# The kernels' transform of an attention + S4D program: its last stage on sixteen 32x32 tiles

## The chip, the cores and the metric

The program runs on one core of a Trainium2 chip. A core has five engines that run in parallel and each take their instructions in order: TensorE (PE in the profile, its weight loads PEld), VectorE (DVE), ScalarE (ACT), GpSimd (POOL) and SyncE (SP, which here only issues transfers). TensorE writes its results to PSUM, 128 partitions with eight banks of 512 float32 values each; DVE and ACT empty the banks. The metric is the device time of one execution in microseconds (us), lower is better.

## What is computed

The reference applies two kinds of layer in turn, each on a layer norm of x (2048 rows, 640 columns) and added to x: attention with 32 heads, and an S4D convolution; then both again with the same weights.

```python
A = -exp(log_A_real) + 1j * A_imag;  C = (C_real + 1j * C_imag) * dt[:, None]
P = exp((A * dt[:, None])[:, :, None] * pos)          # 640 channels, 128 states, 2048 positions
K = 2.0 * einsum("dn,dnl->dl", C, P).real             # one kernel of 2048 taps for each channel
y = irfft(rfft(u, 2L) * rfft(K, 2L))[:L] + u * D_skip # causal convolution, channel by channel
x = x + attn(norm(x)); x = x + s4d(norm(x)); x = x + attn(norm(x)); x = x + s4d(norm(x))
```

The convolution is done as a transform of u, a product with the transform of K, and a transform back. K does not depend on x, so its transform is made once and serves both S4D layers.

## The kernel before, in words

**The stages.** In order of time: the first attention (queries and keys are projected while the softmax runs; VectorE and TensorE build the taps K beside it, `kgen`, and store them in DRAM as `kd`); the output projection of the first attention (`out_proj`), with the transform of K (`ktransform`) in the same stretch; the first convolution (`ssm`); the second attention; the second convolution.

**What sets the order.** Inside the attention the order on every engine is written out by hand: a planner (`Plan`, `fill`, `slot`, `weave`) keeps a clock for TensorE, ScalarE and VectorE and ties each instruction to the one before it. `weave` takes steps of `kgen` (a step ends at each `yield`) while the planned VectorE is not ahead of the planned TensorE by 0.2. Some small steps wait in a list `slow`; each has a number k and is taken at the latest when `expand(k)` begins. Outside the attention, so in `out_proj`, `ktransform` and `ssm`, no such ties are made: a list scheduler orders the instructions when the program is built, those written earlier first where several are ready, and each engine then runs its list in order. `ktransform` is written between the two halves of row 2 of `out_proj` (the call `weave(1000)`), so its instructions come ahead of those of the rows behind.

**`out_proj`.** Sixteen rows s of 128 positions. A row is loaded (`otl`), split in two parts (`oh` by ScalarE, `ol` by VectorE), multiplied by the two parts of the weights in 30 matmuls of 320 columns (tile `po`, two banks `M`), added to x, normed, and cut into `uh` and `ul`, which the convolution reads.

**`ktransform`.** Five blocks b of 128 channels, one after the other:

1. The taps of the block, `kl` (128 x 2048), come from `kd` in one transfer of 1 MB, a block ahead, into one of two buffers. The skip weight is added to tap 0. Sixteen transposes (tile `pkt`, two banks `T`) turn it; ScalarE writes the high part `ktrh` (scaled by `ksc`), VectorE the low part `ktrl`.
2. Eight groups of twelve matmuls with the constants `e1` (tile `pkx`, two banks `X`), each copied into `kx1` (`x1` in the code; ScalarE six, VectorE two). The copies lay four channels side by side.
3. The last stage, in eight steps q: four transposes of `kx1` (`pkt`), ScalarE writes `kxt` with the scale, one 128x128 matmul of 512 columns with the constant `f2` (tile `pkf`, two banks `F`), and VectorE takes its result apart with two `stream_shuffle`s: the first sixteen rows of each 32 twice into `kn0`, the second sixteen twice into `kn1`; ScalarE then gives half of `kn1` the other sign (`sgn`). After every second step two transfers of 512 KB store `kn0` in `kha` and `kn1` in `khb` (DRAM).

So `kha` and `khb` hold each half of the result doubled: the convolution multiplies its own transform by the one, and its transform with rows exchanged (`SWAP`) by the other.

**`ssm`.** For each block of channels eight steps q; in `stage2b` a step loads `ka` and `kb` (256 KB each, from `kha` and `khb`, one piece of 2 KB for each partition; three buffers) and VectorE and GpSimd multiply by them.

**Bound.** The scale `ksc` is made once from the largest absolute values of C and the skip weights: three `reduce_max` on VectorE into `kbig` (written in one step of `kgen`, with the end of the first `expand`), one `partition_all_reduce` on GpSimd, and seven small VectorE instructions (`bound`).

Of the kernel before, what the change touches and what calls it, by code (L numbers as in the profile page):

```python
# [21 lines left out]
P = 128  # L22
L = 2048
# [64 lines left out]
def mha_s4d_kernel(ctx, tc, x_in, wqkv, wo, lar, aim, cr, ci, ldt, dsk,  # L88
                   c_e1, c_eb, c_f2, c_fa, c_sel, c_lv, c_id, c_sg, c_e16, c_f16, c_id16, c_dn, out, parts="asas", general=None):
# [22 lines left out]
    def pst(pool, *a, **k):  # L112
        return ps_[pool].tile(*a, **k)
# [4 lines left out]
    kha = dram.tile([P, D // 4, P], F32, name="kha")  # L118
    khb = dram.tile([P, D // 4, P], F32, name="khb")
# [72 lines left out]
    def kgen():  # L192
# [166 lines left out]
        for n, t in enumerate((ld["cr"], ld["ci"], skip)):  # L359
            ve.reduce_max(big[:, n:n + 1], t, axis=AX.X, apply_absolute_value=True)  # L360
# [12 lines left out]
        slow.append((1, bound))  # L373
        load_powers(2)
        yield
# [815 lines left out]
    ups = []  # L1191
# [17 lines left out]
    DUP0 = list(range(16)) * 2  # L1209
    DUP1 = list(range(16, 32)) * 2  # L1210

# [3 lines left out]
    def ktransform(e1):  # L1215
# [4 lines left out]
        f2 = c1.tile([P, P], F32, name="f2")  # L1220
        sy.dma_start(f2, c_f2)
        sgn = c1.tile([P, 1], F32, name="sgn")
        sy.dma_start(sgn, c_sg)

        skip = c1.tile([P, NCT], F32, name="skip")
        sy.dma_start(skip, dsk)

        def load(b):
            kl = c2.tile([P, L], F32, name="kl")
            sy.dma_start(kl, kd[b * P:b * P + P, :])  # L1230
            return kl
        kls = [load(0)]

        def unit_load(b):
            kl = kls.pop()
            if b + 1 < NCT:
                kls.append(load(b + 1))
# [3 lines left out]
            for i4 in range(4):  # L1241
                pt = pst("T", [P, 4, P], F32, tag="T", name="pkt")
# [6 lines left out]
            x1 = c1.tile([P, 32, NI // 2, 16], F32, name="kx1")  # L1249
            for i2 in range(NI // 2):  # L1250
# [6 lines left out]
                (ve.tensor_copy if i2 % 4 == 1 else se.copy)(by_channel(x1, i2), ps.rearrange("p r i (g c) -> p (r i) g c", c=4))  # L1257
                yield
            prev = None
            for q in range(9):  # L1260
                if q < 8:
                    pt = pst("T", [P, 4, P], F32, tag="T", name="pkt")
                    for g in range(4):
                        te.transpose(pt[:, g, :], x1[:, 4 * q + g].rearrange("p i s -> p (i s)"), ident)
                    xt = c2.tile([P, 512], F32, name="kxt")
                    se.activation(xt, pt.rearrange("p g k -> p (g k)"), AF.Copy, scale=ksc[:, 1:2])
                if prev is not None:
                    g0 = b * 32 + 4 * (q - 1)
                    if q % 2:
                        kn = [c2.tile([P, 2, 512], F32, name=f"kn{s}") for s in range(2)]  # L1270
                    px = pst("F", [P, 512], F32, tag="F", name="pkf")
                    te.matmul(px, f2, prev, start=True, stop=True)  # L1272
# [3 lines left out]
                    if q % 2 == 0:  # L1276
                        for s, dst in enumerate((kha, khb)):
                            sy.dma_start(dst[:, g0 - 4:g0 + 4, :].rearrange("p g k -> p (g k)"),
                                         kn[s].rearrange("p q k -> p (q k)"))
                prev = xt  # L1280
                yield
        for b in range(NCT):
            yield from unit_load(b)
# [65 lines left out]
    def ssm(x, uh, ul, consts, last):  # L1349
# [19 lines left out]
        with ExitStack() as c:  # L1369
# [29 lines left out]
            def stage2b(b, q, xt):  # L1399
# [3 lines left out]
                sy.dma_start(ka, kha[:, g0:g0 + 4, :].rearrange("p g k -> p (g k)"))  # L1403
                sy.dma_start(kb, khb[:, g0:g0 + 4, :].rearrange("p g k -> p (g k)"))
# [227 lines left out]
def _constants():  # L1632
# [13 lines left out]
    for s, o, m in ((0, 0, C), (1, 0, S), (0, 1, -S), (1, 1, C)):  # L1646
        fa[:, s, :, :, o] = np.einsum("hli,cd->hlcid", m.reshape(4, 4, 16), e4)
    f2 = f2.reshape(2, NI // 2, 2, 4, P).transpose(1, 0, 2, 3, 4)
    sg = np.zeros((4, 2, 16, 1))
    sg[:, 0], sg[:, 1] = -1.0, 1.0  # L1650
# [5 lines left out]
    cs = dict(c_e1=e1.reshape(P, -1), c_eb=eb.reshape(P, -1), c_f2=f2.reshape(P, P), c_sg=sg.reshape(P, 1),  # L1656
              c_fa=fa.reshape(P, -1), c_sel=sel.reshape(P, -1), c_lv=lv, c_id=np.eye(P))
    cs = {n: np.ascontiguousarray(a.astype(np.float32)) for n, a in cs.items()}
    for n, a in (("c_e16", e1), ("c_f16", f2)):
# [11 lines left out]
          "c_e1", "c_eb", "c_f2", "c_fa", "c_sel", "c_lv", "c_id", "c_sg",  # L1671
# [31 lines left out]
```

## Time and profile before

| | |
|---|---|
| time, median of 3 runs (lowest to highest) | 2678.65 us (2678.31 to 2682.86) |
| the profiled execution: its time, its span | 2680.85 us, 2679.1 us |
| busy in the span: PE, ACT, DVE, POOL | 94%, 88%, 57%, 31% |
| first attention ends, `out_proj` begins | about 1103 us into the span |
| first to last transpose of `kl`; last shuffle of `pkf` | 1133.4 to 1229.7 us; 1249.5 us |
| first matmul of the first convolution | 1273.6 us |
| last load of `ka` in the second convolution | 2653.9 us |

Times in the answers of the trace are microseconds from the start of the span, and mean times of one instruction are in nanoseconds (ns). In a row of a group stand line, engine, operation, what is written and what is read, shapes and count, then busy time and the mean of one, then the idle time of the engine just before them. Line 78 is the wrapper through which the ScalarE, VectorE, GpSimd and SyncE calls go, so such rows are told apart by their tiles. In a timeline, "x16" means sixteen instructions of one kind in a row, with the start of the first and the time to the end of the last. A float32 matmul appears as two instructions, one for each pass. The ends of matmuls are modelled, so it is the distance from start to start that tells what one costs.

### The profile page before, as it was taken

The numbers are of one execution on the slowest core, as the hardware profiler recorded it, in microseconds if no ns is written. First come the engines' busy times: TensorE is split into PE (matmuls) and PEld (weight loads), VectorE is DVE, ScalarE is ACT, GpSimd is POOL, SyncE is SP. The second block draws the span as 40 slices with busy tenths as digits, with TensorE's granted clock in tenths as the row PEclk, the third lists the DMA queues.
The fourth block names the chain that finished last, engine by engine and source line by source line (L and its number), as shares of the span: only waits on it lengthen the run. The fifth ranks groups of instructions, "written<-read, shape, count | busy, mean of one in ns | idle before, by whom it ended". The sixth has DMA issues, their size and how long they took to land.

```text
span 2679.1 us, 116332 instructions
## 1 busy us (share of the span) xinstructions
PE 2530.0 (94%) x51106; PEld 1425.0 (53%) x51106; DVE 1516.0 (57%) x3451; ACT 2368.7 (88%) x2793; POOL 827.7 (31%) x1256
## 2 busy tenths in 40 slices
PE   7899999999999998899998999999999998999898
PEld 3445444444444443678896444454444443444788
DVE  8687777886855994477776333232233221154865
ACT  7889999999999999676655799999999999999564
POOL 1123323333323334301672122222222222222376
PEclk9999999999999999999999999999999999999999
DMA  6513222322221224364542121121121113222465
GB/s 210 181 49 86 67 76 55 87 55 76 52 61 49 54 68 155 110 233 162 189 151 69 40 59 50 50 58 47 45 65 38 54 30 93 69 67 60 145 190 162
DMA packets 186580, 242.18 MB, mean 90 GB/s; under 512 B 43376, under 2 KB 128976, under 8 KB 184400
## 3 DMA queue, kind: packets, MB, share of 16 engines
q1 hardware_dynamic: 150048, 188.35, 21.8%
q0 software_dynamic: 36016, 46.30, 7.0%
q8 instruction: 403, 6.60, 1.0%
q14 instruction: 113, 0.93, 0.1%
HBM read 158.50 MB, written 76.01 MB: 88 GB/s over the span
## 4 chain that ended last, share of the span: by engine, by line
ACT 52%; PE 25%; issue 10%; DVE 6%; DMA 3%; POOL 1%; SPq 0%; ACTq 0%; DVEq 0%; POOLq 0%
ACT pt L78 50%; PE pa L892 4%; PE psv L1419 3%; PE psy L1429 3%; PE S L858 3%; PE psx L1407 2%; PE m L611 1%; PE psx L1384 1%; PE po L1312 1%; DMA kop<-ks 1%; PE pst L1394 1%; PE pkf L1272 1%; DVE ktab L78 1%; PE po L1307 1%; PE pq L764 1%
## 5 line engine op out<-in xcount | busy, mean ns | idle before, releaser
L78 ACT ACTIVATE pt<-S 128x1024 f32<-128x1024 f32 x2048 | 1928.6, 1032 | 41.4 <-PE S L858 29.2
L892 PE MATMUL pa<-pt,V 64*32 64x512 f32 x16384 | 1100.9, 590 | 1.4 <-DVE oc L78 1.2
L858 PE MATMUL S<-qop,kop 61*32 61x512 f16 x16384 | 882.9, 381 | 85.2 <-ACT pt L78 68.4
L858 PEld LDWEIGHTS <-kop 61*32 61x32 f16 x16384 | 366.7, 89 | 741.1 <-issue 622.4
L892 PEld LDWEIGHTS pa<-pt,V 64*32 64x32 f32 x16384 | 315.1, 106 | 74.6 <-issue 9.7
L78 POOL DMA_DIRECT2D dn<-oc x252 | 124.5, 501 | 670.6 <-DVE oc L78 643.8
L78 DVE TENSOR_SCALAR qc<-m 128x512 f32<-128x512 f32 (+1 forms) x68 | 46.8, 689 | 303.6 <-PE m L611 303.6
L78 POOL DMA_DIRECT2D db<-dn x252 | 128.0, 514 | 135.1 <-DMA dn<-dr 132.1
L78 DVE COPY oc<-pa 128x512 f32<-128x512 f32 x64 | 44.1, 690 | 199.6 <-PE pa L892 191.9
L611 PE MATMUL m<-xh,wh 64*32 64x512 f16 x2560 | 147.9, 379 | 5.5 <-DVE qc L78 5.5
L78 POOL DMA_DIRECT2D ot<-oc x256 | 130.4, 516 | 71.6 <-DVE oc L78 42.8
L611 PE MATMUL m<-xh,wl 64*32 64x512 f16 x2560 | 148.1, 377 | 0.0
L611 PE MATMUL m<-xl,wh 64*32 64x512 f16 x2560 | 146.7, 376 | 0.0
L611 PEld LDWEIGHTS <-wh 64*32 64x32 f16 x5120 | 92.9, 93 | 78.4 <-issue 36.4
L78 ACT COPY xt<-pst 128x1024 f16<-128x1024 f16 x80 | 81.6, 1022 | 47.2 <-PE pst L1394 47.0
L1412 POOL TENSOR_TENSOR t<-t,kb 128x512 f32<-128x512 f32 x80 | 102.0, 1276 | 67.6 <-DVE t L78 66.7
L78 POOL DMA_DIRECT2D dn<-dr x63 | 35.3, 560 | 248.8 <-DVE dr L78 236.4
L78 DVE TENSOR_SCALAR V<-m 128x160 f32<-128x160 f32 x64 | 20.7, 324 | 158.5 <-PE m L577 158.5
L78 DVE TENSOR_TENSOR kb<-ktab 128x512 f32<-128x512 f32 x160 | 107.7, 692 | 0.0
L577 PEld LDWEIGHTS <-xh 128*128 128x128 f16 x960 | 79.7, 98 | 47.0 <-issue 31.6
L1413 POOL TENSOR_TENSOR t<-t,t 128x512 f32<-128x512 f32 x78 | 99.3, 1273 | 8.5 <-DVE t L78 2.6
L329 PEld LDWEIGHTS m<-kb,ka 128*32 128x32 f32 x3840 | 61.0, 109 | 72.1 <-issue 55.3
(305 smaller groups left out, 4020.7 us busy)
## 6 DMA issues: line engine op xcount, KB each, us to landing
ka<-kha SPq DMA_DIRECT2D x80, 256.0 KB
kb<-khb SPq DMA_DIRECT2D x80, 256.0 KB
db<-dn POOLq DMA_DIRECT2D x252, 64.0 KB, 2.6
kop<-ks SPq DMA_DIRECT2D x176, 80.0 KB
kpw<-wd POOLq DMA_DIRECT2D x60, 192.0 KB, 4.7
qop<-qs SPq DMA_DIRECT2D x256, 40.0 KB
ot<-oc POOLq DMA_DIRECT2D x256, 40.0 KB, 3.0
kha<-kn SPq DMA_DIRECT2D x20, 512.0 KB
```

The source lines that it names most:

```text
L78: made = f(out, *a, **k)
L329: chain(te.matmul(ps[32 * j:32 * j + 32, c8, :], a[n][:, ch, :], b[n][:, dd, :], start=(n == 0), stop=(n == 2), tile_position=(0, 32 * j)))
L577: chain(te.matmul(ps[:, :n], a_[:, ct, sl], m[:, ct, :], start=(k == 0), stop=(k == 14)))
L611: chain(te.matmul(ps[r][32 * t:32 * t + 32, :], a_[rows, ct, 32 * u:32 * u + 32], m[rows, ct, 512 * v:512 * v + 512], start=(k == 0), stop ...
L764: te.matmul(pq, a_[:, ct, :], m[:, ct, sl], start=(n == 0), stop=(n == 14))
L858: chain(te.matmul(S[32 * t:32 * t + 32, 512 * r:512 * r + 512], kt_[rows, kc + 32 * t:kc + 32 * t + 32], qt[rows, :], start=True, stop=Tru ...
L892: chain(te.matmul(pa[r][32 * j:32 * j + 32, :], V[rows, kt, VP * h:VP * h + 32], pts[j // 2][rows, 512 * (j % 2):512 * (j % 2) + 512], sta ...
L1407: te.matmul(px, f2[:, f, :], xt[:, k, :], start=(n == 0), stop=(n == 2))
L1412: ge.tensor_mul(t2, t2, kb)
L1413: (ge if g0 else ve).tensor_add(t1, t1, t2)
L1419: te.matmul(pv[:, g].rearrange("p r i c -> p (r i c)"), t1[:, g * P:g * P + P], fa, start=True, stop=True)
L1429: te.matmul(py[:, i, :], eb[:, 4 * i4 + i, r, :], v[:, r, 4 * i4 + i].rearrange("p g c -> p (g c)"), start=(r == 0), stop=(r == 1))
```

## The change

- **Last stage of `ktransform`.** `kx1` is laid out so that the channels of one residue (channel modulo 4) have 32 partitions of the transposed tile to themselves. `f2` becomes two 32x32 matrices for each group of 32 rows: one gives the first half of the result already doubled, the other the second half doubled and with its signs. `turned(t)` makes the sixteen transposes of half a block (now in the banks `X`, shared with `pkx`; each reads with a step of 32 elements) and four ScalarE writes of `kxt`. `ends(t, xt, s, dst)` issues sixteen 32x32 matmuls of 512 columns, four row groups times four column groups, into four banks (`F0` to `F3`, one buffer each), two copies by VectorE and two by ScalarE into `kn`, and two transfers of 512 KB. It is called four times a block. The two shuffles, the ScalarE sign and the constant `sgn` with its load are gone; the banks `T` are gone in this stretch.
- **`kl`.** One buffer instead of two, allocated with the projection weights; the first block is loaded while the first attention still runs, each later one after the sixteen transposes of the block before, in four transfers of 32 channels each (256 KB), which put the channels in the new order. The skip weights are loaded in that order too.
- **`kha`, `khb`** change layout, so `ka` and `kb` are read in pieces of 512 bytes, four for each partition, instead of one of 2 KB.
- **Bound.** A `yield` before each of the three `reduce_max`; `bound` stands behind the loads of `load_powers(2)` in `slow`, with number 3 instead of 1.

```diff
         for n, t in enumerate((ld["cr"], ld["ci"], skip)):
+            yield
             ve.reduce_max(big[:, n:n + 1], t, axis=AX.X, apply_absolute_value=True)
...
-        slow.append((1, bound))
         load_powers(2)
+        slow.append((3, bound))
...
+            kl0[:] = [w1.tile([P, L], F32, name="kl")]
+            rest.append(lambda: load_kl(0))
...
+    def load_kl(b):
+        for ch in range(4):
+            sy.dma_start(kl0[0][32 * ch:32 * ch + 32, :],
+                         kd[b * P:b * P + P, :].rearrange("(g c) l -> c g l", c=4)[ch])
...
-                pt = pst("T", [P, 4, P], F32, tag="T", name="pkt")
+                pt = pst("X", [P, 4, P], F32, tag="X", name="pkt")
...
+            if b + 1 < NCT:
+                load_kl(b + 1)
-            x1 = c1.tile([P, 32, NI // 2, 16], F32, name="kx1")
+            x1 = c1.tile([P, 4, NI // 2, 4, 32], F32, name="kx1")
...
-                    te.matmul(px, f2, prev, start=True, stop=True)
-                    for s in range(2):
-                        ve.stream_shuffle(kn[s][:, (q - 1) % 2, :], px, [DUP0, DUP1][s])
-                    se.activation(kn[1][:, (q - 1) % 2, :], kn[1][:, (q - 1) % 2, :], AF.Copy, scale=sgn)
...
+            def turned(t):
+                xt = c2.tile([P, 4, 4, P], F32, name="kxt")
+                for q in range(4):
+                    pt = pst("X", [P, 4, P], F32, tag="X", name="pkt")
+                    for g in range(4):
+                        te.transpose(pt[:, g, :], x1[:, :, :, :, 16 * t + 4 * q + g].rearrange("p c i s -> p (c i s)"), ident)
+                    se.activation(xt[:, q], pt, AF.Copy, scale=ksc[:, 1:2])
+                return xt
+
+            def ends(t, xt, s, dst):
+                px = [pst("F", [P, 512], F32, tag=f"F{ch}", name=f"pkf{ch}") for ch in range(4)]
+                for ch in range(4):
+                    rows = slice(32 * ch, 32 * ch + 32)
+                    for g in range(4):
+                        te.matmul(px[ch][32 * g:32 * g + 32, :].rearrange("p (q k) -> p q k", k=P), f2[rows, s, :],
+                                  xt[rows, :, g, :], start=True, stop=True, tile_position=(32 * ch, 32 * g))
+                for h in range(2):
+                    kn = c2.tile([P, 2, 4, P], F32, name=f"kn{s}")
+                    for ch in range(2):
+                        (se.copy if ch else ve.tensor_copy)(kn[:, ch], px[2 * h + ch].rearrange("p (q k) -> p q k", k=P))
+                    sy.dma_start(dst[2 * b + t][:, 2 * h:2 * h + 2], kn)
+            xts = [turned(0)]
+            for t in range(2):
+                yield
+                ends(t, xts[t], 0, kha)
+                yield
+                if t == 0:
+                    xts.append(turned(1))
+                yield
+                ends(t, xts[t], 1, khb)
...
-                sy.dma_start(ka, kha[:, g0:g0 + 4, :].rearrange("p g k -> p (g k)"))
-                sy.dma_start(kb, khb[:, g0:g0 + 4, :].rearrange("p g k -> p (g k)"))
+                for t, src in ((ka, kha), (kb, khb)):
+                    sy.dma_start(t.rearrange("p (g k) -> p g k", k=P),
+                                 src[g0 // 16].rearrange("(g a) c q k -> (a c) g q k", g=4)[:, :, q % 4])
...
-                    psum(c3, M=2, T=2, F=2)
+                    psum(c3, M=2, F=1)
```

More of the change, by code (lines that the diff above doesn't have):

```diff
@@ L88, in mha_s4d_kernel @@
 def mha_s4d_kernel(ctx, tc, x_in, wqkv, wo, lar, aim, cr, ci, ldt, dsk,
-                   c_e1, c_eb, c_f2, c_fa, c_sel, c_lv, c_id, c_sg, c_e16, c_f16, c_id16, c_dn, out, parts="asas", general=None):
+                   c_e1, c_eb, c_f2, c_fa, c_sel, c_lv, c_id, c_e16, c_f16, c_id16, c_dn, out, parts="asas", general=None):
     nc = tc.nc
@@ L117, in mha_s4d_kernel @@
     wd = dram.tile([P, 3, len(LV), D], F32, name="wd")
-    kha = dram.tile([P, D // 4, P], F32, name="kha")
-    khb = dram.tile([P, D // 4, P], F32, name="khb")
+    kha = dram.tile([2 * NCT, P, 4, 4, P], F32, name="kha")
+    khb = dram.tile([2 * NCT, P, 4, 4, P], F32, name="khb")
     qs = dram.tile([2, D, L], F16, name="qs")
@@ L1219, in ktransform @@
         c2 = c.enter_context(tc.tile_pool(name="f2", bufs=2))
[L1220 to L1223, printed above, removed]
+        f2 = c1.tile([P, 2, 32], F32, name="f2")
+        sy.dma_start(f2, c_f2.rearrange("p (s m) -> p s m", s=2))
         skip = c1.tile([P, NCT], F32, name="skip")
[L1226 to L1232, printed above, removed]
+        sy.dma_start(skip, dsk.rearrange("(g c) n -> c g n", c=4))
+        kls = kl0
         def unit_load(b):
-            kl = kls.pop()
-            if b + 1 < NCT:
-                kls.append(load(b + 1))
+            kl = kls[0]
             ve.tensor_add(kl[:, 0:1], kl[:, 0:1], skip[:, b:b + 1])
@@ L1260, in unit_load @@
-            for q in range(9):
-                if q < 8:
-                    pt = pst("T", [P, 4, P], F32, tag="T", name="pkt")
+            def turned(t):
+                xt = c2.tile([P, 4, 4, P], F32, name="kxt")
+                for q in range(4):
+                    pt = pst("X", [P, 4, P], F32, tag="X", name="pkt")
                     for g in range(4):
[L1264 to L1272, printed above, removed]
-                    for s in range(2):
-                        ve.stream_shuffle(kn[s][:, (q - 1) % 2, :], px, [DUP0, DUP1][s])
-                    se.activation(kn[1][:, (q - 1) % 2, :], kn[1][:, (q - 1) % 2, :], AF.Copy, scale=sgn)
[L1276 to L1280, printed above, removed]
-                yield
```

18 lines of the change are left out of this document (9 added, 9 removed).

## The prediction

> **What bounds the kernel now.** First the page: its first line and its line of engines.
>
> ```profile
> span 2679.1 us, 116332 instructions
> PE 2530.0 (94%) x51106; PEld 1425.0 (53%) x51106; DVE 1516.0 (57%) x3451; ACT 2368.7 (88%) x2793; POOL 827.7 (31%) x1256
> ```
>
> Those are averages over unlike stages, so next the busy times by stretch around the change (columns: PE, PEld, DVE, ACT, POOL, granted clock, DMA share, GB/s): projection rows alone, rows with the kernels' transform, the rest of the rows, the first convolution.
>
> ```profile
> 1103.00:1133.00 30.00, 28.30 (x184) 26.92 (x184) 21.44 (x54) 11.78 (x17) 15.34 (x22) 1.00 0.49 154
> 1133.00:1248.00 115.00, 113.34 (x927) 86.86 (x927) 87.55 (x238) 89.10 (x145) 6.34 (x6) 1.00 0.56 212
> 1248.00:1289.00 41.00, 37.79 (x348) 35.30 (x347) 31.73 (x84) 23.70 (x40) 10.03 (x7) 1.00 0.41 141
> 1289.00:1416.00 127.00, 125.32 (x1312) 111.61 (x1311) 92.93 (x223) 77.65 (x144) 99.64 (x79) 1.00 0.50 158
> ```
>
> In the transform's 115 us PE is busy for 113, VectorE and ScalarE for three quarters. The chain that ended last says the same: the transform's matmuls, and then rows of the projection with nothing else between them.
>
> ```profile
> 1238.45 0.86 PE pkf L1272 x2
> ...
> 1248.20 2.92 PE po L1312 x20
> 1251.12 1.58 PE po L1307 x10
> ```
>
> So work taken from PE here should shorten the stage, as long as rows can be pulled into the time that comes free: the rows after 1248 were ready to run but stood behind the transform.
>
> **The last stage, what goes.** Two views: PE's timeline inside block 1's last stage, and the groups of the 115 us.
>
> ```profile
> 1170.00 1.02 PE L1272 MATMUL pkf<-kxt,f 128*128 128x512 f32 x2
> 1170.86 0.60 PE L1264 MATMUL pkt<-ident,kx 128*128 128x128 f32 x4
> 1171.30 1.08 PE L1272 MATMUL pkf<-kxt,f 128*128 128x512 f32 x2
> ```
>
> ```profile
> L1272 PE MATMUL pkf<-kxt,f 128*128 128x512 f32 x80 | 41.3, 608 | 0.0
> L78 ACT ACTIVATE kn<-kn,sgn 128x512 f32<-128x512 f32 x38 | 27.0, 721 | 1.5 <-DVE kn L78 0.9 <-DVE va L78 0.2
> L78 ACT ACTIVATE kxt<-pkt,ksc 128x512 f32<-128x512 f32 x40 | 26.6, 677 | 8.8 <-PE pkt L1264 8.8
> L78 ACT COPY kx<-pkx 128x512 f32<-128x512 f32 x30 | 17.4, 584 | 6.4 <-PE pkx L1256 6.3
> L78 DVE STREAM_SHUFFLE kn<-pkf 128x512 f32<-128x512 f32 x77 | 52.2, 737 | 0.0
> L78 DVE COPY kx<-pkx 128x512 f32<-128x512 f32 x10 | 6.9, 686 | 3.2 <-PE pkx L1256 3.2
> ```
>
> A step takes 1.30 us of PE: 0.86 for the two passes of the matmul (its start to the next transposes), 0.44 for four transposes (1170.86 to 1171.30). The matmuls that go are 5 blocks x 8 x 0.86 = 34.4 us. The 160 transposes stay; that they now read with a step I cost at nothing, and a tenth on each (0.011 us) would be 1.8 us.
>
> **What comes.** Twenty calls of `ends`, each sixteen float32 tiles of 512 columns. The trace has no such call; the nearest are the attention's matmuls on eight 64x32 tiles, and one sum over four 32x32 tiles.
>
> ```profile
> 791.56 1.04 PE L892 MATMUL pa<-pt,V 64*32 64x512 f32 x16
> 792.42 0.40 PE L858 MATMUL S<-qop,kop 61*32 61x512 f16 x8
> 792.76 0.24 PE L577 MATMUL m<-vh,xh 128*128 128x160 f16 x1
> ...
> 793.18 0.23 PE L577 MATMUL m<-vh,xh 128*128 128x160 f16 x1
> 793.25 0.23 PE L577 MATMUL m<-vl,xh 128*128 128x160 f16 x1
> 793.41 0.41 PE L858 MATMUL S<-qop,kop 61*32 61x512 f16 x8
> 793.64 1.04 PE L892 MATMUL pa<-pt,V 64*32 64x512 f32 x16
> ...
> 155.66 0.40 PE L539 MATMUL m<-sq,sel 32*32 32x512 bf16 x4
> 155.98 0.89 PE L858 MATMUL S<-qop,kop 61*32 61x512 f16 x16
> ```
>
> Eight float32 tiles (sixteen instructions, two passes each) take 0.86 us together, the time of one: tiles run side by side. Four 32x32 tiles in four row groups do too: 0.32 us to the next kind, about one pass of 0.23. And changing between tile shapes costs: from the scores to another tiled kind 0.23 us, to a 128x128 kind 0.34; from 128x128 back 0.16 instead of the 0.07 between two of its own. So about 0.1 us each way. An estimate for one `ends`: 0.86, some 0.1 for starting twice as many tiles, 0.2 for two changes of shape: 1.15 us, and 23.0 for twenty. **PE saves 34.4 - 23.0 = 11.4 us.** Bounds: 15 if calls stand together and change no shape; -4 if no more than eight tiles ever run side by side (20 x (1.72 + 0.2) = 38.4). I take the estimate, since rows and columns of tiles each show no loss.
>
> The Trainium skill (TensorEngine Tiling (Array Packing), Key Properties) says that a change of tiling mode drains TensorE, which speaks against small groups of tiles between 128x128 work. Taken at its word, each of forty changes would cost the tail of a matmul, 0.608 less the 0.43 between two passes, 0.18 us, and 7 us in all; the rows above show a change at half of that, 4 us, and the sum goes by them.
>
> **What empties the banks.** VectorE loses 80 shuffles of 0.737 (59 us) and gets 40 copies of 0.686 (27); ScalarE loses 40 signs of 0.721 (29) and gets 40 copies of 0.584 (23). Both were behind PE, so this is worth nothing by itself. But the banks are single now. After an `ends` two copies an engine must end, about 1.4 us, before the next `ends` may write. Of the three such waits in a block the first is covered by the sixteen transposes of `turned(1)` (1.8 us); two are bare: 2.8 us. And `ends` needs all four writes of `kxt`: 4 x 0.677 plus 0.6 for the first transposes, 3.3 us, of which the transposes fill 1.8: 1.5 bare. Together 4.3 us a block, **22 us in all, if nothing else is put there**. What can be put there is row matmuls (25 us of them stand after 1248: 2.92 + 1.58 for each row) and the next block's transposes. I take 3 us lost, with 0 and 22 as ends: rows were ready, and the scheduler did put them into the gaps of the present order.
>
> **Loads and stores.** `kl` in four transfers waits for the block's transposes and lands while 96 matmuls and the last stage run, some 20 us; price 0 (if that cover went, each block would wait for 1 MB). On SP it stands ahead of the stores of `kn` and the loads `otl`; four issues of 0.4 us delay them by 1.6 us, against two row buffers. The constant `sgn` leaves SP just ahead of `skip`, for which the first block waits:
>
> ```profile
> 1130.03 0.61 SPq L78 DMA_DIRECT2D sgn<-in_c_sg  x1
> ```
>
> **-0.6 us** (0 to -0.6). `ka` and `kb` in 512-byte pieces: the packets of a row load (all of 512 bytes, two microseconds from 1133) against those of `ka` and `kb` (20 us from 1360), and the lead of one load over its use.
>
> ```profile
> q1 hardware_dynamic: 656, 0.33, 54.7%
> ...
> q1 hardware_dynamic: 1612, 2.94, 46.1%
> ```
>
> ```profile
> 1334.45 0.32 SPq L78 DMA_DIRECT2D kb<-khb  x1
> 1334.87 0.38 SPq L78 DMA_DIRECT2D ka<-kha  x1
> ```
>
> ```profile
> 1342.57 0.67 DVE L78 TENSOR_TENSOR t<-psx,ka 128x512 f32<-128x512 f32 x1
> ```
>
> 0.547 x 2 us x 16 / 656 = 27 ns for 512 bytes; 0.461 x 20 x 16 / 1612 = 92 ns for, mostly, 2 KB. A pair of loads becomes 1024 x 27 ns / 16 = 1.7 us, against a lead of 7.7 us (the same number in both orders). Price 0; each 0.1 us that the 80 pairs came late would be 8 us.
>
> **The bound.** On the attention's start ScalarE, its bottleneck, waits for scores that wait for VectorE, and the three maxima lie on that chain.
>
> ```profile
> 133.58 1.52 DVE kbig L78 x3
> ```
>
> ```profile
> 138.03 1.02 ACT L78 ACTIVATE pt<-S 128x1024 f32<-128x1024 f32 x1 [4.78 <-PE S L858]
> ```
>
> With the `yield`s the planner can put the emptying of `m` first. Worth up to 1.5 us of ScalarE's 4.8; I take **1.0** (0 to 1.5), as the planner's clock does not know that VectorE was late.
>
> **The sum**: 11.4 - 3 + 0.6 + 1.0 = 10.0 us less. The profiled execution took 2680.85 (span 2679.1 and 1.75 around it), 2.2 above the median; against it the forecast is 2670.85, against the median of 2678.65 it is 2668.7.
>
> **The rivals.** What a measurement can tell from no change is 0.2%, 5.4 us: 2673.3 to 2684.0.
>
> 1. *The waits stay empty (slower).* The scheduler sets the order before the run. If it takes the sixteen tiles for sixteen matmuls in a row, PE looks full to it, it lines up the four `ends` of a block and puts no row between; on the chip PE then stands idle at `pkf`, and the rows come after as now. Price: all 22 us, so 2678.65 + 22 - 11.4 - 1.6 = 2687.7. It decides from 13 us of empty waits on. For it: the attention, full of such tiles, is ordered by hand with a clock of its own. Against: nothing in the present order shows a misjudged stretch, but nothing in it is tiled either.
> 2. *ScalarE takes over the last stage.* It has 8 x 0.677 + 8 x 0.584 = 10.1 us a block there, PE had 8 x 1.30 = 10.4. If that stage stays as long as ScalarE and nothing moves in, the gain is 5 x 0.3 = 1.5 us and 1.6: 2675.5. For it: the bare waits; against: ScalarE is busy for only 89 of 115 us. The Trainium skill (TensorEngine Tiling (Array Packing), PSUM Bottleneck) speaks for this one: tiling speeds up TensorE and leaves the emptying of PSUM as it was.
> 3. *Only eight tiles run side by side*: 2678.65 + 4 + 3 - 1.6 = 2684. Against it stand the rows above; sixteen float32 tiles are not among them.
> 4. *The short pieces come late*: slower by 8 us and more; the leads speak against it.
>
> **How the numbers follow.** Forecast 0.52, rival 1 0.26, rival 2 0.15, rival 3 0.04, rival 4 0.03. The time is the forecast's, 2668.7, with its own range of 2662 to 2674 (waits of 0 to 8 us, 15 us saved at most). The range of 8 in 10 reaches over rivals 2 and 3 to just beyond rival 1: 2660 to 2689. Faster: the forecast but for its edge, and a little of rival 2, 0.53; within: most of rival 2, half of rival 3 and the part of rival 1 near its turning point, 0.19; slower 0.28.
>
> **What would show it.** In the profile after: the sixteen-tile groups `pkf` start within 0.1 us and the next kind 1.1 to 1.2 us later (wrong, if 1.9 or more); the waits of PE for copies out of `pkf` add up to 3 us (rival 1: over 13); the rows left after the last `ends` take no longer than now; the first convolution starts 9 us earlier after the attention; no wait for `ka` or `kb`; ScalarE's gap near 135 us is 3.3 to 4.8 us. The prediction is wrong if the stage from the attention's end to the convolution does not shorten, or if the attention or the convolutions move by more than 2 us.

## The result, and the profile after

The kernel after takes 2701.09 us (median of 5 runs, 2695.70 to 2704.51), the kernel before, run beside it, 2679.00 us (2678.31 to 2682.86). The ratio is 1.0076, with a 95% interval of 1.0061 to 1.0091: slower by 0.8%. The forecast was 2668.7 us, and the range ended at 2689.

The first line of the page after and its line of engines:

```profile
span 2699.3 us, 117384 instructions
PE 2534.6 (94%) x51666; PEld 1422.0 (53%) x51666; DVE 1487.5 (55%) x3331; ACT 2365.6 (88%) x2793; POOL 824.5 (31%) x1256
```

VectorE and ScalarE have lost work as expected, PE has not. The busy times by stretch, cut at the same events as for before (rows alone, rows with the transform, the other rows, first convolution; columns as there, the granted clock after POOL):

```profile
1104.20:1134.20 30.00, 27.73 (x181) 26.38 (x180) 20.92 (x53) 11.75 (x17) 15.39 (x22) 1.00 0.50 153
1134.20:1269.40 135.20, 120.76 (x1516) 87.75 (x1516) 67.35 (x129) 88.64 (x149) 8.65 (x7) 0.97 0.56 187
1269.40:1306.70 37.30, 34.08 (x328) 31.43 (x321) 28.66 (x74) 21.05 (x36) 7.55 (x5) 1.00 0.48 159
1306.70:1433.70 127.00, 125.35 (x1312) 111.63 (x1311) 93.00 (x224) 77.65 (x144) 99.40 (x79) 1.00 0.54 159
```

The transform's stretch is 20 us longer, with PE idle for 14.4 us in it (1.7 before) and the granted clock below one. The first convolution is unchanged: 125.35 us of PE in 127, against 125.32. PE's timeline in block 0's last stage shows the new groups and where they stand:

```profile
1150.72 1.14 PE L1274 MATMUL pkf<-kxt,f 32*32 32x512 f32 x32
1151.80 1.16 PE L1265 MATMUL pkt<-ident,kx 128*128 128x128 f32 x8
1152.89 1.04 PE L1274 MATMUL pkf<-kxt,f 32*32 32x512 f32 x2
1153.86 0.71 PE L1265 MATMUL pkt<-ident,kx 128*128 128x128 f32 x4
1154.50 1.13 PE L1274 MATMUL pkf<-kxt,f 32*32 32x512 f32 x30
1156.45 1.60 PE L1274 MATMUL pkf<-kxt,f 32*32 32x512 f32 x32 [0.81 <-DVE kn L78]
1158.36 1.69 PE L1274 MATMUL pkf<-kxt,f 32*32 32x512 f32 x32 [0.32 <-DVE kn L78]
```

The first group runs as forecast: the next kind starts 1.08 us after it. The order puts the last four transposes behind the first tile of the second group; they wait for a bank that ScalarE empties into `kxt`, and the group's rest waits with them. The second, third and fourth then stand one behind the other with no row between; the third and the fourth wait for the copies out of the single banks, and even a group that has begun is stretched to 1.6 us, because its later tiles find their bank still full. The groups of the stretch say the same, with the idle time before each:

```profile
L1274 PE MATMUL pkf<-kxt,f 32*32 32x512 f32 x640 | 33.9, 614 | 5.7 <-DVE kn L78 4.1 <-ACT kn L78 1.6
L1265 PE MATMUL pkt<-ident,kx 128*128 128x128 f32 x160 | 24.7, 292 | 3.4 <-ACT kxt L78 3.4
L1241 PE MATMUL pkt<-ident,kl 128*128 128x128 f32 x80 | 13.5, 306 | 5.8 <-DVE ktrl L78 5.0 <-DVE kl L78 0.9
L78 DVE COPY kn<-pkf 128x512 f32<-128x512 f32 x39 | 25.6, 687 | 40.1 <-PE pkf L1274 30.6 <-DMA khb<-kn 5.9 <-issue 3.6
L78 ACT COPY kn<-pkf 128x512 f32<-128x512 f32 x39 | 21.7, 587 | 18.3 <-PE pkf L1274 7.7 <-DMA khb<-kn 6.1 <-ACT kn L78 4.5
```

Twenty groups are busy for 33.9 us where 20 x 1.14 = 22.8 would do: 11 us are waits inside them (0.9 of it is half clock in one group, see the last section). With the 14.4 - 1.7 = 12.7 us of idle time that is 24 us lost, against the 11.4 saved. Three causes in these rows were in no step of the prediction. VectorE and ScalarE wait 12 us for the stores of `kn` (two buffers for each). PE waits for `ktrl`, which stands behind those copies (ahead of the wait for it near 1164, VectorE stands 2.1 us for a store). And PE waits for `kxt`, which stands on ScalarE behind the `u` and `uh` of the rows and two copies of `kn`. The chain shows such a store on the path, and then the rows that stood behind the transform as before:

```profile
1212.67 5.36 DMA khb<-kn
...
1270.44 2.93 PE po L1321 x20
```

### The profile page after: what moved, and what is told of

Its sections match the earlier page's. It is cut to its first block, busy times and chain, and to the rows that moved or that the text cites. A ratio compares the mean times of both kernels' runs of the same rounds, so it can differ in the third digit from the quotient of the medians.

```text
span 2699.3 us, 117384 instructions
## 1 busy us (share of the span) xinstructions
PE 2534.6 (94%) x51666; PEld 1422.0 (53%) x51666; DVE 1487.5 (55%) x3331; ACT 2365.6 (88%) x2793; POOL 824.5 (31%) x1256
## 4 chain that ended last, share of the span: by engine, by line
ACT 51%; PE 26%; issue 10%; DVE 5%; DMA 4%; POOL 1%; SPq 0%; ACTq 0%; DVEq 0%; POOLq 0%
ACT pt L78 49%; PE pa L893 4%; PE S L859 3%; PE psv L1429 3%; PE psy L1439 2%; PE psx L1417 2%; PE m L612 2%; PE po L1321 2%; PE psx L1393 1%; PE pst L1403 1%; PE pkx L1255 1%; PE po L1316 1%; DMA kop<-ks 1%; PE pkt L1265 1%; PE pq L765 1%
```

## The experiments

The theories, by the numbers that the expectations use. **Theory 1**: the order puts the groups back to back on single banks and leaves the rows for later. A **rival**: the stores of `kn` hold up the copies. Another: the tiles or the changes of shape cost it themselves. **Theory 3** came with the first results: ScalarE does the rows' `u` and `uh` ahead of the copies. Ten of the kernels below are changes of the kernel after, two of the kernel before, and one is the kernel after once more. To compare them within one execution the table gives the **stage**: from the first row matmul of the first projection (`po`) to the last `psx` group of the first convolution. Its two ends are the first start in the row of the tile `po` and a row of PE's timeline; in the kernel after, 1104.0 and 1429.04. The ratio is to the kernel before, run beside each (medians 2679.0 to 2680.2 us). One profile was taken of each kernel, so a stage is one execution, and two of one program differ by 4.5 us (after and after again).

| kernel | time, us | ratio to before, 95% interval | stage, us |
|---|---|---|---|
| before (first runs) | 2678.65 | | 308.4 |
| after | 2701.09 | 1.0076 (1.0061 to 1.0091) | 325.0 |
| after, again | 2700.81 | 1.0082 (1.0068 to 1.0095) | 329.5 |
| after, edit of bound undone | 2696.56 | 1.0059 (1.0045 to 1.0074) | 326.6 |
| before, only the edit of bound | 2680.72 | 1.0001 (0.9992 to 1.0010) | 308.4 |
| after, half of the stores left out | 2698.37 | 1.0056 (1.0042 to 1.0070) | 324.1 |
| after, u on VectorE | 2693.83 | 1.0054 (1.0040 to 1.0067) | 323.6 |
| before, u on VectorE | 2682.39 | 1.0010 (1.0000 to 1.0020) | 310.8 |
| order by hand | 2710.59 | 1.0102 (1.0086 to 1.0118) | 335.8 |
| order by hand, u on VectorE | 2687.66 | 1.0029 (1.0019 to 1.0038) | 311.6 |
| the same, pieces of four | 2678.15 | 0.9994 (0.9985 to 1.0003) | 306.2 |
| the same, pieces of three | 2689.07 | 1.0035 (1.0023 to 1.0048) | 315.1 |
| pieces of four, pkx divided | 2681.06 | 0.9999 (0.9991 to 1.0008) | 307.5 |
| the same, edit of bound undone | 2679.31 | 0.9996 (0.9987 to 1.0006) | 307.2 |
| fewer, larger pieces, edit of bound undone | 2675.53 | 0.9982 (0.9973 to 0.9991) | 301.1 |

**The order by hand.** The transform gives way after each piece, the row matmuls from the seventh row on are tied into PE's order with it, and every five of them let one piece pass. The last two groups of a block move behind the first transposes of the next.

```diff
-            xts = [turned(0)]
-            for t in range(2):
-                yield
-                ends(t, xts[t], 0, kha)
...
+            turn(1, xts[1], 0)
+            ends(0, xts[0], 0, kha)
+            yield
+            turn(1, xts[1], 1)
+            yield
+            turn(1, xts[1], 2)
+            ends(0, xts[0], 1, khb)
+            yield
+            turn(1, xts[1], 3)
+            late.append(lambda: ends(1, xts[1], 0, kha))
+            late.append(lambda: ends(1, xts[1], 1, khb))
```

> The kernel after, with the order of the last stage written out by hand from the seventh row on: five row matmuls between every two pieces of the transform, the two groups of sixteen tiles of a half never back to back, and those of the second half moved behind the next block's first transposes. All operations and sizes are those of the kernel after. Theory 1 (TensorE stands idle because the order puts the groups back to back and leaves the rows for later): after lost 16.6 us on the groups and the waits behind them against the 23.0 forecast, and 10 us on other waits in the stretch; with rows in between at least 15 of these come back, so 2672 to 2687 against 2701. Rival (the tiles themselves cost it, by their shape or by the changes between tile shapes, of which this order has more): no gain, 2698 or more. Rival (stores of kn that hold up the copies are the whole of it): the groups are further apart here, so the stores have time, and the same gain as theory 1 would follow; the run without half of the stores tells those two apart.

It took 2710.59 us, 9.5 more than after. So a place for the rows between the groups was not enough. By its number alone this is the rival that the tiles themselves cost it; the waits and the later orders speak against that. ScalarE's timeline of this kernel in block 1, and PE's beside it:

```profile
1194.55 0.58 ACT L78 COPY kn<-pkf 128x512 f32<-128x512 f32 x1
1197.15 1.73 ACT L78 ACTIVATE u<-x,nb,rs 128x640 f32<-128x640 f32 x2 [2.01 <-DVE nb L78]
1198.79 1.33 ACT L78 CAST uh<-u 128x640 f16<-128x640 f32 x2
1200.03 0.57 ACT L78 COPY kn<-pkf 128x512 f32<-128x512 f32 x1
```

```profile
1197.05 1.06 PE L1275 MATMUL pkf<-kxt,f 32*32 32x512 f32 x8 [0.18 <-DVE kn L78]
1200.66 1.93 PE L1275 MATMUL pkf<-kxt,f 32*32 32x512 f32 x8 [2.55 <-ACT kn L78]
```

Between two copies of one group ScalarE stands at `u` for 2.01 us, waiting for VectorE's `nb`, and then does `u` and `uh` of two rows, 3 us. The bank stays full, and PE, whose order is fixed, stands with it. Four such stretches hold PE up for 10.2 us. In before ScalarE waited 5.2 us for `nb` between 1135 and 1270, and PE waited for ScalarE for 0.6 us there; now single banks hang on ScalarE. A new theory came from this: the rows' work on ScalarE, ahead of the copies.

**Half of the stores.**

```diff
-                ends(t, xts[t], 1, khb)
+                ends(t, xts[t], 1, None)      # makes the tiles and copies, stores nothing
...
-                for t, src in ((ka, kha), (kb, khb)):
+                for t, src in ((ka, kha), (kb, kha)):
```

> The kernel after without the stores of the second of the two doubled results (its sixteen tiles and its copies stay); the convolutions load the first result in its place, so part of the output is another. Order of TensorE as after. If the waits of VectorE and ScalarE for the stores of kn (6.1 + 5.9 us in the transform) are what empties TensorE, 2689 to 2695, that is 6 to 12 us below after. If the order by itself empties it (back to back groups on single banks), the copies come earlier but the banks are still single and the rows still stand behind: 2697 to 2701, less than 4 us gained.

The waits for the stores are gone, and the time, 2698.37 us, lies where it was expected if the order empties PE (2697 to 2701), 3.4 us above what was expected if the stores do. By the ratio it is 5 us below after, but the intervals overlap. The stage's row, with that of after above it:

```profile
1104.00:1291.30 187.30, 170.59 (x1846) 135.34 (x1840) 104.48 (x226) 110.10 (x181) 29.43 (x32) 0.98 0.53 174
```

```profile
1101.60:1287.90 186.30, 174.26 (x1846) 135.42 (x1840) 104.02 (x226) 110.23 (x181) 29.41 (x32) 0.95 0.39 119
```

(Both from the first row to the first `psx`.) PE is idle for 12.0 us instead of 16.7, but the granted clock fell from 0.98 to 0.95, and PE is busy for 3.7 us more with the same instructions. So the stores do hold the copies up, but they are not the whole, and part of what their absence brought was lost to the clock. What they cost by themselves these runs don't tell.

**The kernel after once more.**

> The kernel after once more, for a second profile of the same program. If the granted clock at half behind a wait depends only on the wait, the same two stretches as before (near 1164 and 1188, 3.4 us lost) come again. If it also depends on where the wait falls in some window that is not the program's, the stretches lie elsewhere or are longer, with the same waits, and the times of the runs scatter by some us as they did (2695.7 to 2704.5). Median 2697 to 2704 by both.

The median is the same, 2700.81 us. PE waits at the same places for about as long, but the clock isn't the same. Here is the same work in both executions, from the end of the second block's wait for `kxt` on, in after (first two fences) and in after again:

```profile
1183.70 0.71 PE L1265 MATMUL pkt<-ident,kx 128*128 128x128 f32 x4 [1.72 <-ACT kxt L78]
```

```profile
1183.70:1195.70 12.00, 10.86 (x131) 6.52 (x131) 6.95 (x11) 7.31 (x12) 0.35 (x1) 0.86 0.80 317
```

```profile
1177.92 0.71 PE L1265 MATMUL pkt<-ident,kx 128*128 128x128 f32 x4 [1.72 <-ACT kxt L78]
```

```profile
1177.92:1189.92 12.00, 10.95 (x116) 5.17 (x117) 5.38 (x9) 5.93 (x10) 0.34 (x1) 0.57 0.78 309
```

In after again the clock is at half for 10.2 of these 12 us, in after for 3.4, and in after again PE gets through fewer instructions (116 instead of 131).

Over the whole stage, from first row to first `psx`, the second execution has a clock of 0.94, PE is busy for 5.5 us more with the same instructions, and it is 4.5 us longer:

```profile
1099.50:1291.30 191.80, 176.05 (x1846) 137.51 (x1840) 104.44 (x226) 110.28 (x181) 29.43 (x32) 0.94 0.52 170
```

The first row also comes at 1099.5 instead of 1104.0: the start of this stage moves by 4.5 us between two executions of one program. This bears on every comparison of single profiles here.

**The bound's edit**, undone in after and made alone in before:

```diff
         for n, t in enumerate((ld["cr"], ld["ci"], skip)):
-            yield
             ve.reduce_max(big[:, n:n + 1], t, axis=AX.X, apply_absolute_value=True)
...
+        slow.append((1, bound))
         load_powers(2)
-        slow.append((3, bound))
```

> The kernel after with the edit of bound undone (no yield between the three maxima, its second part due at 1 and ahead of the load of the powers, as in before). In after ScalarE's gap near 135 us was 5.38 us against 4.78 before, and the first row came 1.2 us later. If the edit causes it: 2699.9, 1.2 us below after, with the gap at 4.8 us. If it is chance: no difference, gap 5.4. By the prediction's price it would be 1.0 us above after.

> The kernel before with only the edit of bound (a yield ahead of each of the three maxima, the second part due at 3 and behind the load of the powers). By the prediction 2677.7 (1.0 us less than 2678.65, ScalarE's gap near 135 us at 3.3 to 4.3 us); if the later attention of after came from it, 2679.9 (gap 5.4 us); if neither, no difference.

Alone it does nothing that can be measured: 1.0001 (0.9992 to 1.0010), which leaves room for 2.1 us of gain and 2.7 of loss. Undone in after, it came out 4.5 us lower, but the intervals overlap, and its profile's stage is no shorter. Undone in the hand order (below), it is within the interval as well. ScalarE's gap near 135 us was longer in after, but it differs between executions of one program: 5.38 us in after, 3.69 in after again, 3.62 in after with the edit undone, and 4.16 in before with the edit alone (4.78 without). So it tells nothing of the edit.

**u on VectorE.** `u` and its float16 copy from the seventh row on; in after, in the hand order, and as a control in before.

```diff
-            se.copy(uh[:, s, :], u)
+            (se.copy if on_act else ve.tensor_copy)(uh[:, s, :], u)
...
-                        ln_u(x, i0, m, ln_stats(lambda i: x[:, i0 + i, :], m), uh, ul, up2, not general)
+                        ln_u(x, i0, m, ln_stats(lambda i: x[:, i0 + i, :], m), uh, ul, up2, not general and (n > 0 or i0 < 6))
```

> The kernel after; from the seventh row on the normalised row u and its float16 copy uh are made by VectorE instead of ScalarE. TensorE's order is as in after. Theory 3 (ScalarE does u and uh, some 3.1 us for two rows, ahead of the copies kxt and kn for which TensorE waits): the waits of TensorE for kxt (3.4 us at 1.7 each, in the second and fourth block of after) go, and with them what the lower clock behind them costs: 2692 to 2697 against 2701. Theory 1 alone (the banks are single and the groups stand back to back): the waits for kn stay, no more than 2 us gained: 2698 to 2701.

> The kernel before with u and uh of the rows from the seventh on made by VectorE: a control. In before TensorE did not wait for ScalarE or VectorE in the transform (1.4 us idle in 115), so nothing is to be had there: within 3 us of 2679.9. If it gained as much as the kernel after did (7 us), the gain would be of the rows and not of the groups' waits.

> The hand order again, with u and uh of the rows from the seventh on made by VectorE, and with the last block's last two groups ahead of the last row instead of behind it. In the hand order each of four blocks had one idle stretch of 2.55 us, ScalarE standing at u for nb with a copy of pkf behind it, and the granted clock was at half for some 6 us after each; the convolution after it was 10 us longer with two more such stretches. Theory 3 with theory 1: these go, 31 us less than the hand order at most (4 x 2.55 + 11.9 + 10), so 2680 to 2690, at or below after by over 10. If the tiles themselves are what costs, or the copies of pkf are too slow whatever the order, it stays above 2695.

After gains 7 us, with PE's order unchanged up to the last rows. The ratio is 1.0054 (to 1.0067) against 1.0082 (from 1.0068) of after again on the same chip; it overlaps that of after's first runs, and the profiled stage is shorter by 1.4 us than in after and by 5.9 than in after again. The waits of PE for `kxt` (3.4 us in after) are gone, those for `kn` stay:

```profile
PE pkf L1274 <- ACT kn L78: 3.3, 4, 0.8
PE pkf L1274 <- DVE kn L78: 2.4, 6, 0.8
```

Before gains nothing (1.0010). This control isn't a clean one, as the scheduler also gave PE another order in it: the first `psx` starts at 1246.0, ahead of the last rows. The hand order gains 23 us and is now 13 below after; PE's 10.2 us of waits for ScalarE at `pkf` are gone. So ScalarE's rows ahead of the copies are a cause, and with them out of the way the order by hand brings another 6 us (with the last block's groups moved ahead of the last row). Together they give back over half of the 22 us. What was left shows in PE's and ScalarE's timeline at the start of the convolution:

```profile
1286.40 0.22 PE L1421 MATMUL psx<-uh,e1s 128*128 128x128 f16 x1 [4.41 <-DVE x L78]
```

```profile
1285.04 2.05 ACT L78 CAST x<-psx 128x512 f16<-128x512 f32 x4 [3.97 <-DMA khb<-kn]
```

The last stores of `kn` had not landed when the convolution wanted to write `x` where `kn` had stood.

**Smaller pieces.** The order is moved towards an earlier end, with four or three row matmuls for each piece, and then with `pkx` divided.

```diff
-                if s >= 6:
-                    weave(1)
...
         def row_mm(s, *a, **k):
+            if s >= 6:
+                if count[0] % 4 == 0:
+                    weave(1)
+                count[0] += 1
...
+                if i2 in (1, 3, 5, 7):
+                    space[0] = 2 if i2 < 7 else 3
+                    yield
```

> The hand order with u and uh on VectorE from the seventh row on, with four row matmuls between two pieces instead of five and eight behind a block's last kl transposes, so that the last groups stand two rows before the end of the projection. In hand_dve three things were left: TensorE waited four times 1.44 us for ktrl ahead of pkx, and 4.41 us at the start of the convolution, because the last stores of kn had not landed when the convolution wrote where kn had stood. Theory 1 with theory 3: both go, some 8 us less than hand_dve, so 2676 to 2682, level with before or just below. If the row pieces are now too short to cover the copies (a group, 0.59 + 0.45 us of other work, and a group again against 1.4 us of copies), 0.4 us for each of ten pairs comes back: 2682 to 2686.

> The same with three row matmuls between two pieces. The cover of a pair of neighbouring groups falls by another 0.15 us, and that of the other copies too: 0 to 4 us above hand2 if TensorE's order has to cover the copies, level with hand2 if the copies no longer bind.

> The order of hand2 with the 96 pkx matmuls of a block in four pieces, two row matmuls behind each of the first three and three behind the last, and six instead of eight behind the last kl transposes. In hand2 the groups of sixteen tiles and their waits take 21.7 us together, about the 23.0 of the forecast, but TensorE waited 7.7 us inside the pkx matmuls (0.8 in before), for the copies of kx. Theory 1 with theory 3: some 5 of these go, 2671 to 2676, faster than before. If the copies of kx only move the wait elsewhere (ScalarE and VectorE as the bound of the stage, rival 2 of the forecast): level with hand2, 2677 to 2680.

> The same, with the edit of bound undone. By the prediction's price of that edit 1.0 us above the run with it; if the edit makes the first attention later, as the runs of after against the run with it undone would have it (4 us, their intervals overlap), up to 4 us below; by the run of before with that edit alone, no difference.

With four the time is level with before (0.9994), 23 us below after: the whole loss is back. With three it is 11 us slower again, where 0 to 4 were expected. The cover is too thin ahead of `pkx`. PE waits for `ktrl` for 5.1 us (0.3 with four), and behind the longest of these waits the clock is at half for 6.8 us, which costs up to 3.4. That is 8.2 of the 8.9 us by which the stage is longer.

```profile
PE pkx L1260 <- DVE ktrl L78: 5.1, 6, 2.6
```

```profile
1214.00:1220.00 6.00, 4.98 (x51) 4.72 (x48) 2.15 (x3) 1.60 (x3) 2.05 (x2) 0.51 0.98 200
```

To divide `pkx` (theory 1 said 5 us) gave nothing: 0.9999 and, with the edit of bound undone, 0.9996. PE's waits for `kx` inside `pkx` only fell from 3.8 to 3.1 us.

**Fewer, larger pieces.** Where the 10 us of gain that were forecast had gone was still open. In the fine order a return to the rows costs, as PE's timeline of the kernel with `pkx` divided and the edit of bound undone shows:

```profile
1176.36 0.40 PE L1327 MATMUL po<-woh,oh 128*128 128x320 f32 x1
1176.60 0.31 PE L1327 MATMUL po<-wol,oh 128*128 128x320 f32 x1
1176.74 0.30 PE L1327 MATMUL po<-woh,oh 128*128 128x320 f32 x1
```

The first row matmul behind another kind takes 0.24 us to the next, the others 0.14 to 0.15. The last kernel has transposes in eights and rows in pieces of six to eight.

```diff
-                if i4 == 3:
-                    space[0] = 6
-                yield
+                if i4 % 2:
+                    if late:
+                        late.pop(0)()
+                    space[0] = 8
+                    yield
```

> The order of hand4 (with the edit of bound undone) in fewer and larger pieces: eight transposes instead of four at a time and six to eight row matmuls behind them, ten returns to the rows in a block instead of fifteen. In the fine orders the first row matmul behind transposes costs 0.23 to 0.25 us to the next instead of 0.147, and the waits and extra starts between row matmuls add up to 7.9 us (2.5 in before). If it is the returns that hold back the rest of the gain: 25 fewer x 0.09 = 2 us less than hand4 with the edit undone, 2674 to 2679. If the copies into the two banks X bind (eight transposes fill both): level or above, 2679 to 2684.

It takes 2675.53 us, 0.9982 of before (0.9973 to 0.9991): faster than both kernels, 25.6 us below after and 3.8 below before. PE's timeline between two groups, the row of the twenty groups, and the stage in two stretches:

```profile
1174.53 1.14 PE L1278 MATMUL pkf<-kxt,f 32*32 32x512 f32 x32
1175.60 1.16 PE L1270 MATMUL pkt<-ident,kx 128*128 128x128 f32 x8
1176.52 1.42 PE L1329 MATMUL po<-woh,ol 128*128 128x320 f32 x8
1177.87 1.14 PE L1278 MATMUL pkf<-kxt,f 32*32 32x512 f32 x32
```

```profile
L1278 PE MATMUL pkf<-kxt,f 32*32 32x512 f32 x640 | 23.4, 600 | 0.2 <-DVE kn L78 0.2
```

```profile
1100.00:1130.60 30.60, 27.49 (x186) 26.36 (x180) 21.46 (x56) 11.69 (x17) 15.64 (x22) 1.00 0.49 151
1130.60:1263.50 132.90, 128.27 (x1661) 103.02 (x1662) 88.45 (x186) 84.79 (x148) 15.46 (x11) 1.00 0.62 207
```

The groups wait for 0.2 us in all (5.7 in after) and are busy for 23.4 (33.9 in after), and the clock stays at one. From the first row to the first `psx` it takes 163.5 us, where before takes 170.7:

```profile
1102.90:1273.60 170.70, 167.34 (x1287) 138.72 (x1281) 128.17 (x346) 113.19 (x181) 29.59 (x32) 1.00 0.51 185
```

That is 7.2 us, and PE is busy for 11.6 us less, which is the 11.4 of the forecast. The rest went into waits between other kinds (7.7 us idle instead of 3.4). The medians differ by 3.8 us, and the interval reaches to 7.2. The interval overlaps that of the pieces of four, so that these pieces gain over those isn't shown; and whether it would be the returns, or the longer cover of the copies, this run doesn't separate: both changed. The kernel before was not run with an order by hand; with 3.4 us idle here it has little to gain by one.

## Why the prediction was wrong

The step that failed is **"I take 3 us lost, with 0 and 22 as ends: rows were ready, and the scheduler did put them into the gaps of the present order."** It was near 24 us: 11 inside the groups and 13 idle (in the rows above 5.7 at the groups, 3.4 for `kxt`, 5.8 ahead of the `kl` transposes; 1.7 were idle before). Rows were ready, but the scheduler's order did not put them there; orders by hand with `u` and `uh` on VectorE did, and then the loss was gone. That is the pattern of rival 1, which had 0.26, was to decide from 13 us of empty waits on, and named the groups in a row (four; here it is three). Its price, 2687.7 us, was 13 too low. That the scheduler counts sixteen tiles as sixteen matmuls in a row, as rival 1 has it, fits this order, but no run tested it.

Point by point:

- **34.4 us of matmuls less, 23.0 us of groups more: right.** Sixteen float32 tiles run side by side, 1.07 to 1.08 us to the next kind; with 0.1 to 0.2 for the changes of shape that is 1.15 to 1.25, where the sum had 1.15. Where hardly a group waits (the last kernel), the twenty are busy for 23.4 us, and PE's busy time in the stage falls by 11.6 us. Rival 3, only eight at a time, is out: it needed 1.72.
- **Transposes that read with a step, nothing: right.** In the last kernel eight take 0.92 us (1175.60 to 1176.52), 0.115 each, where it was 0.11.
- **The change of shape, 0.1 us each way.** In the last kernel eight row matmuls and the change into a group take 1.35 us (1176.52 to 1177.87), 0.17 more than eight at 0.147; 0.09 of it is the return to the rows. The Trainium skill (TensorEngine Tiling (Array Packing), Key Properties) says that a change of mode drains TensorE, for which the prediction had an estimate of 0.18 us; the measured change in, 0.08, is nearer to the rows' 0.1, and neither decided anything.
- **Bare waits of 4.3 us a block: right in place, too small.** Its three waits are in the timeline. Not in the sum were the waits inside a group, the stores of `kn`, and what stands ahead of the copies on ScalarE. The prediction counted ScalarE's busy time (89 of 115 us) and never its order.
- **The clock: missing.** See the last section. Behind some of the waits it was at half: for 6.8 us of the stage in one execution of after, for 23.9 in the other, where PE is busy for 5.5 us more.
- **`sgn`, -0.6 us: not there.** From the first row to the first transpose of `kl` it takes 30.5 us (1104.0 to 1134.5) where it was 30.6.
- **The bound, 1.0 us: not there.** In after two of the three maxima still run before the emptying of `m`, the gap varies from execution to execution by more than the price, and alone the edit moves nothing that can be measured.
- **`kl` in four transfers, 512-byte pieces: next to nothing, as forecast.** PE waits once for `kl`, 0.9 us, and the convolution is as long as before (rival 4 out).
- **Rival 2**, ScalarE as the bound by its busy time, was not it: a faster stage with the same copies on ScalarE exists (without `u` and `uh`). That ScalarE's order decided was in no rival.

Of the 20.2 us by which the profiled span grew, 16.6 are in the stage (187.3 against 170.7 us to the first `psx`): 24 lost, less the 11.4 saved, and 2.5 more at half clock come to 15 of them. The attention before it ends 1.1 us later, and what follows takes 2.5 us more; the second profile of the same program has the first 3.4 us earlier than before, so this is scatter. The prediction's own test, "if the attention or the convolutions move by more than 2 us", was too sharp for one execution.

## What to carry to other kernels

When banks go from double to single, price the order and not the sum: ask what stands between two uses of a bank on TensorE, and what stands ahead of the copy on each engine that empties it, waits of other work included. A wait that "something will fill" is an assumption about the scheduler; take the empty end as a case of equal weight, or write the order out with the change. Fill with pieces long enough to cover the copies, few enough that the returns don't eat the gain: three, four, and six to eight row matmuls gave 2689, 2678 and 2676 us, the last two with overlapping intervals.

## What the runs showed of the hardware

**The clock can fall behind waits of less than 2 us.** In the kernel after, a wait of 1.90 us in PE's timeline is followed by row matmuls at 0.27 us from start to start instead of 0.147. The busy times in three steps of 3.41 us show the granted clock (third from the end of each row) at half in the second:

```profile
1164.22 0.72 PE L1241 MATMUL pkt<-ident,kl 128*128 128x128 f32 x4 [1.90 <-DVE ktrl L78]
...
1166.80 0.47 PE L1321 MATMUL po<-woh,oh 128*128 128x320 f32 x1
1167.07 0.47 PE L1321 MATMUL po<-wol,oh 128*128 128x320 f32 x1
```

```profile
1161.55:1164.96 3.41, 1.51 (x12) 1.25 (x11) 2.38 (x5) 1.77 (x4) 0.00 (x0) 1.00 1.01 408
1164.97:1168.37 3.40, 3.40 (x18) 3.17 (x18) 2.71 (x5) 1.37 (x2) 0.00 (x0) 0.50 0.50 145
1168.38:1171.79 3.41, 3.41 (x58) 3.22 (x56) 0.95 (x2) 1.57 (x3) 0.00 (x0) 1.00 1.01 215
```

Before had no such stretch in this stage. The traces' record of the clock says more than these rows. In all fifteen traces the stretches at half clock last 3.41, 6.83 or 10.24 us (but for the one with which a record ends), and within an execution they begin a whole number of 3.41 us apart: in after at 1164.97 and 1188.86, which is seven. The idle time of such a step does not decide alone. In after the step from 1182.02, with 1.68 us idle, is followed by full clock and the next one, with 1.14, by half; in after again a step with the same wait of 1.72 us is followed by half clock at once. What else decides these runs don't show.

The Trainium skill (TensorE: Matmul & The Clock Gate, What's actually happening) says that the clock falls to half after an idle window of about 3.4 us, that the windows run free of the kernel, and that it returns after a busy one. The half agrees, and so do the steps of 3.41 us and that the same wait is followed by half clock in one execution and not in another (after and after again). That a whole window has to be idle doesn't agree: single waits of 1.7 to 2.6 us were enough, and the clock stayed down for up to 10 us.
